# Outer magnitudes of an S4 kernel with their weights made as exponentials, and the angle of the weights from one arctangent

## The chip, the cores and the metric

The kernel runs on one core of a Trainium2 chip. The metric is device time in microseconds of one execution, the median over several runs. Five engines take part, each with an instruction stream of its own: PE (matrix products), DVE (vector work), ACT (functions of one argument and copies), POOL and SP. SP issues most of the transfers here, POOL the rest. An engine works through its own instructions in order and waits at an instruction until what it depends on is done.

## The reference, cut to what matters

One block of a network on a sequence x of L = 2048 rows with D = 512 channels. Six vectors come from a condition c; the first half of the block is a long convolution, the second a token mixer with an MLP.

```
mod = (silu(c) @ w_mod)                        # 512 -> 6 x 512: sa, ca, ga, sb, cb, gb
h = layernorm(x) * (1 + ca) + sa
dt = exp(log_dt);  A = A_re + 1j * A_im        # A: 512 x 128
P = exp((dt * A)[:, :, None] * arange(2048))   # 512 x 128 x 2048, complex
K = einsum("dn,dnl,dn->dl", C, P, dt * B).real # 512 x 2048, summed over n = 128
y = irfft(rfft(pad(h.T)) * rfft(pad(K)))[:, :2048].T + h * Dskip
x = x + ga * y
h = layernorm(x) * (1 + cb) + sb
x = x + gb * mixer_mlp(h)                      # w1, shifts by 1 and 2 rows, w2; w3, gelu, w4
```

The change concerns how K is made. K[d, l] = Re of the sum over n of W exp(dt A l), with the weight W = C B dt.

## The kernel before, in words

**How K is tiled.** The exponent is split as l = 64 b + a: an inner factor exp(dt A a) with 64 values of a, and an outer one, W exp(64 dt A b), with 32 values of b. For 16 channels at a time, K is then a set of small products over n (128 rows) of an outer tile e1 (32 columns a channel, real and imaginary part) and an inner tile e0. The 512 channels make 32 steps k of 16 channels; eight blocks t of four steps u, with `t, u = divmod(k, 4)`.

**What a step needs.** Each complex factor is a magnitude times a sine or cosine.

- `turns(k, cos)` makes the phase in turns of both factors as a product on PE (four matmul pairs for the sine, five for the cosine, each on 64 rows, a column range for the inner and one for the outer factor). Tables of constants (C0, C1) multiply rows that hold the phase of each channel, split into a high and a low part (T0S inner, T1S outer). Adding and taking off a large number inside the product (the tiles ON and MG) removes the whole turns. One ACT operation with the table of sines then gives `sn` or `cs`, 128 x 1024.
- `exps(t, u0, u1)`, once a block, makes the magnitudes: four exponentials of 128 x 1024 for the inner factor (p0, one for each step of the block, from TES, the rows of dt A_re), and one of 128 x 768 (p1) that holds for each channel a table of 8 and one of 4 outer exponentials.
- `weigh(t)` multiplies p1's tables of 4 by the magnitudes of the weights, WN, on DVE.
- `products(k)`, on DVE: m1 (the outer magnitude, 16 x 32, as a product of the tables of 8 and 4), e0 from sn, cs and p0 (three operations), e1 from sn, cs and m1 (two operations).
- `burst(k, e0, e1)`: 64 small matmuls that sum over n. Every second step ACT copies the result to KX.

**The loop** runs over k = 0 to 32. In step k the program issues the turns of step k + 2, evictions left from the step before, then the products and the burst of step k. In steps with k % 4 == 1 (called fresh here) the exponentials of the next block come in between: ACT changes its table from sines to exponentials and back there (ACT_TABLE_LOAD). `fill` issues matmuls whose result isn't used, to keep PE at work. Beside this, the loop normalizes x (u_stats, u_norm), takes its short transforms (`u_dft`: 8 matmuls, then two ACT evictions to vs, then transfers to VU by SP), and makes the modulation vectors 3 to 5 (`mod_parts`, `mod_sum`).

**The preparation** in front of the loop: dt; the rows la = dt A_re and tf (phase in turns), split into high and low parts (hilo; `hi` on ACT, `lo` on DVE); `place` and `parts`, products with the placing matrices PA and PB that move the rows to where the loop's products want them (TES, T0S from PA; T1S from PB); the weights wr + i wi = C B; their angle by the arctangent of the smaller over the larger of |wr| and |wi|, with corrections for octant and signs on DVE (at); their magnitude from the sine of that arctangent and a second reciprocal (wn), transposed on PE to WN; and modulation vectors 0 to 2. `load_mod(n)` loads a block of w_mod by SP into one of two buffers "xu", the third block into the buffer of the first; ACT scales it, PE sums it over 128 rows, ACT copies the result (modu).

**What sets the order.** All of this is written out by hand (`manual_schedule`): each engine takes its instructions in the order in which the program issues them. Buffers come from pools. There are two PSUM buffers of 1024 columns for sines, cosines and exponentials alike (xx), two for u_dft and modulation (pu), two for kp.

**Behind the loop**: the skip weights Dskip, loaded into DS at the start, are added to K (`KX`), KX is multiplied by FK (`k_first`), and spectrum, inverse transform and MLP follow. Vs, VU and the loads `ld` are x's way there.

Of the kernel before, what the change touches and what calls it, by code (L numbers as in the profile page):

```python
# [7 lines left out]
F32 = mybir.dt.float32  # L8
# [14 lines left out]
NX0 = 64  # L23
NX1 = 12
NXC = 16 * NX0 + 64 * NX1


def shape_constants():
# [24 lines left out]
    for hh in range(2):  # L53
        for c2 in range(2):
            for cc in range(16):
# [14 lines left out]
    ex1 = np.concatenate([64 * np.arange(8), 512 * np.arange(4)])  # L70
    CE = np.concatenate([(eye[:, :, None] * ex0.reshape(2, 32)[:, None, None, :]).transpose(1, 0, 2, 3).reshape(16, -1),
                         np.zeros((16, 64 * NX1))], 1)
    CE = np.tile(CE, (8, 1))
    for u in range(4):
        CE[u * 32:u * 32 + 32, 1024 + u * 16 * NX1:1024 + (u + 1) * 16 * NX1] = \
            np.tile((eye[:, :, None] * ex1).reshape(16, -1), (2, 1))
    PA = np.zeros((2, 4, 16, 2, 2, 4, 2, 16))
    PB = np.zeros((4, 2, 16, 4, 4, 2, 4, 16))
    for e in range(16):
# [9 lines left out]
        FI=FI.reshape(128, 16 * 128), C0=C0, C1=C1, CE=CE, PA=PA.reshape(128, 512), PB=PB.reshape(128, 2048), ID=np.eye(128)).items()}  # L89
# [20 lines left out]
def body(ctx, tc, A):  # L110
    nc = tc.nc
# [7 lines left out]

    VU = dpool.tile([2, 64, 64, 256], F32, name="VU")  # L120
# [65 lines left out]
    DS = ph.tile([128, 128], F32, name="DS")  # L186
# [5 lines left out]
    CE = ph.tile([128, NXC], F32R, name="CE")  # L192
# [6 lines left out]
    mods = [modu[:, k] for k in range(3)] + [modg[:, k] for k in range(3)]  # L199
# [39 lines left out]

    def exps(t, u0, u1):  # L240
        if u0 == 0:
            PE[t] = [], pe.tile([128, 4, 16, NX1], F32, name="p1")
        p0, p1 = PE[t]
        for u in range(u0, u1):
            x = psx.tile([128, 1024], F32, name="xx")
            if u == 4:
                for i, n in ((0, 512), (512, 64 * NX1)):
                    T.matmul(x[:, i:n], TES[:, t], CE[:, 1024 + i:1024 + n], start=True, stop=True)
                act(p1.rearrange("p u d c -> p (u d c)"), x[:, :64 * NX1], AF.Exp)
                continue  # L250
            l = TES[u * 32:u * 32 + 32, t]
            for i in range(2):
                T.matmul(x[:, i * 512:i * 512 + 512], l, CE[u * 32:u * 32 + 32, i * 512:i * 512 + 512],  # L253
                         start=True, stop=True)
            p0.append(pe.tile([128, 2, 512], F32, name="p0", bufs=6))
            act(p0[u].rearrange("p a b -> p (a b)"), x, AF.Exp)

    def weigh(t):
        q1 = PE[t][1][:, :, :, 8:12].rearrange("p a b c -> p (a b) c")
        V.tensor_mul(q1, q1, WN[:, t * 64:(t + 1) * 64, None].to_broadcast([128, 64, 4]))  # L260
# [9 lines left out]
    cst = pp.tile([128, 512], F32, name="cst")  # L270
# [3 lines left out]
    for k in ("ar", "ai", "cr", "br", "ci", "bi"):  # L274
        raw[k] = pp.tile([128, 4, 128], F32, name="raw_" + k)

# [4 lines left out]
    with tc.manual_schedule():  # L281
# [6 lines left out]
        for k, t in (("PA", PA.rearrange("p a b c -> p (a b c)")), ("CE", CE), ("C0", C0),  # L288
                     ("PB", PB.rearrange("p a b c -> p (a b c)")), ("C1", C1)):
            P.dma_start(t, A[k])  # L290
# [3 lines left out]
        V.memset(DS, 0.0)  # L294
        for j in range(4):
            Y.dma_start(DS[32 * j:32 * j + 1], A["dk"][j:j + 1])
        Y.dma_start(FK, A["FK"])
        V.memset(cst, MAGIC)
        for r in (32, 96):
            V.memset(cst[r:r + 32], 1.0)  # L300
        V.tensor_copy(MG, cst)
        V.memset(cst[:, :384], 0.0)
        for i, (r, v) in enumerate(((0, 1.0), (0, -1.0), (32, 0.25))):
            for q in (r, r + 64):
                V.memset(cst[q:q + 1, i * 128:i * 128 + 128], v)
        V.tensor_copy(ON.rearrange("p a b -> p (a b)"), cst[:, :384])
# [3 lines left out]
        dtp = pp.tile([128, 4], F32, name="dtp")  # L310
        V.tensor_scalar(dtp, dt, INV2PI, None, op0=OP.mult)
# [13 lines left out]
        V.tensor_tensor(as4(la), raw["ar"], by(dt), op=OP.mult)  # L325
        hi(6, la)
        V.tensor_tensor(as4(tf), raw["ai"], by(dtp), op=OP.mult)
# [7 lines left out]
        V.tensor_scalar(ex[:, 4:], ex[:, 4:], 1.0, None, op0=OP.add)  # L335
        V.reciprocal(ex[:, 4:], ex[:, 4:])
        V.tensor_mul(scb, ex[:, 4:], cT)
# [5 lines left out]
        V.tensor_mul(t0, ci, bi)  # L343
        lo(2, t64)
        V.tensor_sub(wr, wr, t0)
# [3 lines left out]
        exps(0, 0, 5)  # L349
        act(C0N, C0.bitcast(F32), scale=-1.0)  # L350
        act(C1N, C1.bitcast(F32), scale=-1.0)
        px = [psx.tile([128, 1024], F32, name="xx") for i in range(2)]

        def parts(i0, i1):
            for v in range(4):
                for i in range(i0, i1):
                    T.matmul(px[v // 2][:, v % 2 * 512:v % 2 * 512 + 512], PB[:, v, i], hilo[:, 2 + i],
                             start=(i == 0), stop=(i == 3))

        parts(0, 2)  # L360
        ax, ay, mn = cr, br, tmp("mn")
# [41 lines left out]
        for i in range(4):  # L403
            s = slice(i * 128, (i + 1) * 128)
            T.transpose(wps[:, s], wn[:, s], ident)
# [636 lines left out]
```

## Time and profile before

| | us |
|---|---|
| median of 3 runs | 812.99 (812.83 to 813.55) |
| the profiled execution | 819.14 |
| its span in the profile | 817.4 |
| preparation | 0 to 42.6 |
| loop of 32 steps | 42.6 to 257.6 |
| spectrum, inverse, mixer, MLP | 257.6 to 817.4 |
| busy over the span: PE | 725.9 (89%) |
| DVE | 511.1 (63%) |
| ACT | 339.0 (41%) |
| POOL | 92.5 (11%) |

The span is the stretch that the profiler recorded of one execution; the time of that execution holds 1.7 us more around it. Busy is the sum of an engine's instructions. The mean granted clock of PE over the span is 0.937 of full speed. Rows of the trace give the start in us, the duration in us, the engine, the line of the kernel, the operation with what it writes and reads, the shape, and in brackets how long the engine stood idle before it and what released it. Groups give the count, then busy time and mean in ns of one, then the idle time before them with the releaser. "PEld" is the load of the fixed operand of a matmul, "SPq" the issue of a transfer by SP. L118 is the helper that issues all of ACT's operations, so ACT's rows are told apart by their tiles.

### The profile page before, as it was taken

The page shows a single profiled execution, that of the slowest core. Times are in us where ns is not written, and L with a number is a line of the kernel's source. Part 1 is how long each engine was busy: PE and PEld are TensorE (multiplying, and loading weights), DVE is VectorE, ACT ScalarE, POOL GpSimd, SP SyncE. Part 2 cuts the span into 40 slices and gives each one's busy share as a digit, 9 for nine tenths or more (in the row PEclk, how much of TensorE's full clock was granted, in tenths as well). Part 3 has the DMA queues.
Part 4 walks back from the last instruction along what each step waited for, and adds up shares of the span by engine and source line. Part 5 has one row for each costly group of instructions (what it writes and reads, how often), then busy time and mean ns, then how long its engine had stood idle before and what let it go on. Part 6 is the DMA issues. An engine that isn't in the chain of part 4 may idle for free. (4 is left out here: it accounts for less than half of the span.)

```text
span 817.4 us, 17349 instructions
## 1 busy us (share of the span) xinstructions
PE 725.9 (89%) x7340; PEld 550.9 (67%) x7340; DVE 511.1 (63%) x883; ACT 339.0 (41%) x540; POOL 92.5 (11%) x186
## 2 busy tenths in 40 slices
PE   3798999889888989999459899999999999999994
PEld 1355555545556956565248788888888888888883
DVE  8999888768765355777479988543526271714211
ACT  3677676656755344453134554221322122222220
POOL 1011111011000000010026331010101010101000
PEclk9999999989998599999769899999999999999997
DMA  8421152421415999495803453010101010101011
GB/s 294 147 53 41 26 145 53 116 68 28 117 40 131 246 250 311 146 307 182 287 1 121 160 177 118 26 53 1 52 1 53 1 52 1 26 1 26 1 26 26
DMA packets 51046, 79.88 MB, mean 98 GB/s; under 512 B 5172, under 2 KB 37816, under 8 KB 49432
## 3 DMA queue, kind: packets, MB, share of 16 engines
q1 hardware_dynamic: 44808, 57.92, 25.6%
q0 software_dynamic: 6160, 20.85, 8.1%
q8 instruction: 58, 0.95, 0.5%
q14 instruction: 20, 0.16, 0.1%
HBM read 52.53 MB, written 26.21 MB: 96 GB/s over the span
## 5 line engine op out<-in xcount | busy, mean ns | idle before, releaser
L871 DVE TENSOR_TENSOR gl<-gf,gh 128x512 fp32r<-128x512 f32 (+1 forms) x48 | 30.4, 644 | 150.5 <-ACT gh L118 150.5
L118 ACT ACTIVATE gf<-pm 128x512 f32<-128x512 f32 (+1 forms) x48 | 27.0, 562 | 182.1 <-PE pm L865 178.4
L865 PE MATMUL pm<-nh,w3l 128*128 128x256 f32 (+1 forms) x352 | 98.5, 280 | 0.0
L864 PE MATMUL pm<-nl,w3h 128*128 128x256 f32 (+1 forms) x352 | 98.5, 280 | 0.0
L863 PE MATMUL pm<-nh,w3h 128*128 128x256 f32 (+1 forms) x352 | 98.4, 279 | 0.0
L876 PE MATMUL pa<-w4h,gh 128*128 128x512 f32 (+1 forms) x176 | 73.8, 419 | 3.2 <-ACT gh L118 0.9
L877 PE MATMUL pa<-w4l,gh 128*128 128x512 f32 (+1 forms) x176 | 69.6, 396 | 0.0
L863 PEld LDWEIGHTS pm<-nh,w3h 128*128 128x128 f32 (+1 forms) x352 | 65.4, 186 | 1.8
L865 PEld LDWEIGHTS pm<-nh,w3l 128*128 128x128 f32 (+1 forms) x352 | 65.4, 186 | 1.1
L864 PEld LDWEIGHTS pm<-nl,w3h 128*128 128x128 f32 (+1 forms) x352 | 65.2, 185 | 0.6
L878 PE MATMUL pa<-w4h,gl 128*128 128x512 f32 (+1 forms) x176 | 64.2, 396 | 0.0
L481 DVE SCALAR_TENSOR_TENSOR e<-sn,p 128x512 f32<-128x512 f32 x64 | 41.3, 686 | 33.5 <-ACT sn L118 14.2
L461 PE MATMUL xx<-MG,ON 64*128 64x512 f32 x160 | 51.0, 416 | 0.0
L462 PE MATMUL xx<-MG,ON 64*128 64x512 f32 x160 | 50.9, 415 | 0.0
L118 ACT ACTIVATE sn<-xx 128x1024 f32<-128x1024 f32 x32 | 32.9, 1027 | 40.9 <-issue 34.4
L884 POOL DMA_DIRECT2D out<-KX x32 | 16.1, 508 | 257.6 <-DVE KX L882 257.5
L876 PEld LDWEIGHTS pa<-w4h,gh 128*128 128x128 f32 (+1 forms) x176 | 33.0, 188 | 17.9 <-ACT gh L118 13.2
L770 PE MATMUL pm<-nl,w1h 128*128 128x256 f32 x128 | 39.0, 305 | 6.6 <-DVE nl L741 6.6
L643 DVE TENSOR_TENSOR ma<-pk,us 128x512 f32<-128x512 f32 x32 | 21.9, 685 | 29.3 <-issue 21.3
L118 ACT ACTIVATE p<-xx 128x1024 f32<-128x1024 f32 (+1 forms) x40 | 37.8, 981 | 5.1 <-PE xx L253 3.3
L501 PEld LDWEIGHTS kp<-e,e 128*32 128x32 f32 x2048 | 30.5, 111 | 13.1 <-issue 8.5
L769 PE MATMUL pm<-nh,w1h 128*128 128x256 f32 x128 | 39.3, 307 | 0.0
(222 smaller groups left out, 1910.7 us busy)
## 6 DMA issues: line engine op xcount, KB each, us to landing
VU<-vs SPq DMA_DIRECT2D x64, 128.0 KB, 2.4
ld<-VU SPq DMA_DIRECT2D x32, 256.0 KB, 8.7
ZT<-z POOLq DMA_DIRECT2D x16, 512.0 KB, 4.4
ld<-ZT SPq DMA_DIRECT2D x16, 512.0 KB, 5.4
wst<-in_w SPq DMA_DIRECT2D x18, 256.0 KB, 3.3
xu<-in_u SPq DMA_DIRECT2D x16, 256.0 KB, 6.6
KX<-in_u SPq DMA_DIRECT2D x16, 256.0 KB, 9.7
GD<-go POOLq DMA_DIRECT2D x16, 256.0 KB, 3.3
```

The costliest lines, as they stand in the source:

```text
L118: return S.activation(out, in_, f, bias=bias, scale=scale)
L461: T.matmul(x[:, :512], la, ma, start=(i == 0), stop=(i == len(ops) - 1))
L462: T.matmul(x[:, 512:], lb, mb, start=(i == 0), stop=(i == len(ops) - 1))
L481: V.scalar_tensor_tensor(e0[:, 1, a], sn[:, 0], 1.0 - 2.0 * a, mg[:, a], op0=OP.mult, op1=OP.mult)
L769: T.matmul(p[:, e], W1h[:, k, c], hi[k], start=(k == 0), stop=False)
L770: T.matmul(p[:, e], W1h[:, k, c], lo[k], start=False, stop=False)
L863: T.matmul(p[:m, e], W3h[:, k, c], hi[k], start=(k == 0), stop=False)
L864: T.matmul(p[:m, e], W3h[:, k, c], lo[k], start=False, stop=False)
L865: T.matmul(p[:m, e], W3l[:, k, c], hi[k], start=False, stop=(k == 3))
L876: T.matmul(acc[i], gh[:m, e, s], W4h[:m, f], start=(f == 0), stop=False)
L877: T.matmul(acc[i], gh[:m, e, s], W4l[:m, f], start=False, stop=False)
L878: T.matmul(acc[i], gl[:m, e, s], W4h[:m, f], start=False, stop=(f == 10))
```

## The change

**Outer magnitudes.** The table of 8 and 4 goes. Instead the logarithm of the weight's magnitude, ln |W|, becomes rows of a product: a new tile TWS holds, in high and low parts, 64 dt A_re (for the outer position) and ln |W|, and its product with C1 (the constants that the outer phase uses too) is the logarithm of the whole weighted outer magnitude. Two more exponentials of 128 x 1024 a block (u = 4, 5) make it for four steps. m1 and `weigh` go, and e1 becomes a single product of 128 x 1024, for which sine and cosine lie in one tile `tr`. CE, the table of constants for the magnitudes, loses its last 768 columns.

**Angle.** arg W = 2 arctan(wi / (|W| + |wr|)), with the sign of wr handled by sw. |W| is exp(0.5 ln(|W| squared)); the same logarithm is ln |W|'s source. One reciprocal is left of three.

**Tables.** `table(i)` issues a load of ACT's table as an instruction of its own, in the place where the program has it. Before, the loads came where the builder put them: in front of the first operation that needs another table.

**Constants.** ON and MG are loaded by POOL as one tile MO instead of being written by memsets on DVE, and MG is one column that is read 512 times. POOL's order of loads changes.

**Order.** In the preparation, C0N, C1N, four of the first six exponentials and the modulation 0 to 2 come behind T1S. The tile of the skip weights, DS, moves behind the loop: a memset and four transfers.

```diff
+    def table(i):
+        S.add_instruction(mybir.InstLoadActFuncSet(name=nc.get_next_instruction_name(), act_func_set_id=i, ins=[], outs=[]))
+
+    LOG, EXP, TRIG = 5, 0, 9
...
-    MG = ph.tile([128, 512], F32R, name="MG")
-    ON = ph.tile([128, 3, 128], F32R, name="ON")
-    WN = ph.tile([128, 512], F32, name="WN")
-    modu = ph.tile([128, 3, 512], F32, name="modu")
...
+    MO = ph.tile([128, 392], F32R, name="MO")
+    ON = MO[:, :384].rearrange("p (a b) -> p a b", a=3)
+    MG = MO[:, 384:385].to_broadcast([128, 512])
+    modu = ph.tile([128, 2, 512], F32, name="modu")
...
     def exps(t, u0, u1):
...
             x = psx.tile([128, 1024], F32, name="xx")
-            if u == 4:
-                for i, n in ((0, 512), (512, 64 * NX1)):
-                    T.matmul(x[:, i:n], TES[:, t], CE[:, 1024 + i:1024 + n], start=True, stop=True)
-                act(p1.rearrange("p u d c -> p (u d c)"), x[:, :64 * NX1], AF.Exp)
-                continue
...
             for i in range(2):
...
+                if u < 4:
+                    r = slice(u * 32, u * 32 + 32)
+                    l, m = TES[r, t], CE[r, i * 512:i * 512 + 512]
+                else:
+                    r = slice(64 - i * 64, 128 - i * 64)
+                    l, m = TWS[r, t * 2 + u - 4], C1[r]
+                T.matmul(x[:, i * 512:i * 512 + 512], l, m, start=True, stop=True)
+            q = pe.tile([128, 2, 512], F32, name="p1" if u > 3 else "p0", bufs=4 if u > 3 else 6)
+            act(q.rearrange("p a b -> p (a b)"), x, AF.Exp)
+            (p1 if u > 3 else p0).append(q)
 
-    def weigh(t):
-        q1 = PE[t][1][:, :, :, 8:12].rearrange("p a b c -> p (a b) c")
-        V.tensor_mul(q1, q1, WN[:, t * 64:(t + 1) * 64, None].to_broadcast([128, 64, 4]))
...
+        act(s2, wr, AF.Square)
+        act(ax, wr, AF.Abs)
+        act(rw, wi, AF.Square)
...
+        V.scalar_tensor_tensor(s2, s2, 1e-37, rw, op0=OP.max, op1=OP.add)
+
+        act(s2, s2, AF.Ln)
+        table(EXP)
+        act(rw, s2, AF.Exp, scale=0.5)
+        V.tensor_add(rw, rw, ax)
+        V.reciprocal(rw, rw)
+        exps(0, 0, 2)
+        table(TRIG)
+        sw = t0
+        V.tensor_scalar(sw, wr, 0.0, -2.0, op0=OP.is_lt, op1=OP.mult)
+        V.tensor_mul(rw, rw, wi)
+        V.scalar_tensor_tensor(rw, sw, 1.0, rw, op0=OP.add, op1=OP.mult)
+        act(at0, rw, AF.Arctan)
...
+        parts(px4, (2, 3, 4, 5), 0, 2)
+        parts(pw4, (6, 7, 0, 1), 0, 2)
...
+        hi(4, ph1)
+        lw = t1
+        V.scalar_tensor_tensor(as4(lw), as4(s2), 0.5, by(ld[:, :4]), op0=OP.mult, op1=OP.add)
+        lo(4, ph1)
+        hi(0, lw)
+        lo(0, lw)
+        parts(px4, (2, 3, 4, 5), 2, 4)
+        table(EXP)
...
+        parts(pw4, (6, 7, 0, 1), 2, 4)
+        for v in range(4):
+            act(TWS.rearrange("p (t v) n -> p v t n", v=4)[:, v], pw4[v].rearrange("p (t n) -> p t n", t=4))
         act(C0N, C0.bitcast(F32), scale=-1.0)
         act(C1N, C1.bitcast(F32), scale=-1.0)
...
+        exps(0, 2, 6)
+        table(TRIG)
         mp = [mod_parts(n) for n in range(2)]
...
     def products(k):
...
-        m1 = wk1.tile([128, 16, 32], F32, name="m1")
-        V.tensor_mul(m1.rearrange("p d (x y) -> p d x y", x=4),
-                     pt[:, :, None, :8].to_broadcast([128, 16, 4, 8]),
-                     pt[:, :, 8:12, None].to_broadcast([128, 16, 4, 8]))
...
-        V.tensor_mul(f2(e1[:, 1]), sn[:, 1], f2(m1))
-        V.tensor_mul(e0[:, 0], cs[:, 0:1].to_broadcast([128, 2, 512]), mg)
-        V.tensor_mul(f2(e1[:, 0]), cs[:, 1], f2(m1))
+            V.scalar_tensor_tensor(e0[:, 1, a], tr[:, 1, 0], 1.0 - 2.0 * a, mg[:, a], op0=OP.mult, op1=OP.mult)
+        V.tensor_mul(e0[:, 0], tr[:, 0, 0:1].to_broadcast([128, 2, 512]), mg)
+        V.tensor_mul(e1.rearrange("p r d x -> p r (d x)"), tr[:, :, 1], m1[:, None, :].to_broadcast([128, 2, 512]))
...
                 if fresh:
+                    table(EXP)
                     exps(k // 4 + 1, 0, 2)
...
-                    for u in range(2, 5):
+                    for u in range(2, 6):
                         exps(k // 4 + 1, u, u + 1)
-                        fill(2)
-                if k % 4 == 3 and k < 28:
-                    weigh(k // 4 + 1)
+                        fill(2 - u // 4)
+                    table(TRIG)
...
+        DS = wml.tile([128, 128], F32, name="wm")
+        V.memset(DS, 0.0)
+        for j in range(4):
+            Y.dma_start(DS[32 * j:32 * j + 1], A["dk"][j:j + 1])
         V.tensor_add(Kq[:, :, :, 31], DS.rearrange("p (h g) -> p h g", h=2), Kq[:, :, :, 31])
```

In each of the following, a row is one instruction, or several alike (x2), with its line, what it writes and reads, and its shape.

ACT at the end of the preparation, from C1N to the first sine of the loop, before (tp_mn is the ratio of which the arctangent is taken, tp_wn the sine of it, hilo the high part of the angle, WN the weights' magnitudes, "xu<-pu" and "modu<-pu" the two halves of a modulation vector):

```order
L118 ACTIVATE C1N<-C_103 128x512
L118 ACT_TABLE_LOAD
L118 ACTIVATE tp_at_295<-tp_mn 128x512
L118 ACT_TABLE_LOAD
L118 ACTIVATE tp_wn<-tp_at_295,hpi 128x512
L118 ACTIVATE xu<-pu 128x512 x2
L118 ACTIVATE modu<-pu 128x512 x2
L118 ACTIVATE hilo<-tp_at 128x512
L118 ACTIVATE T1S<-xx 128x2x4x128 x2
L118 ACTIVATE WN<-pu 128x512
L118 ACTIVATE sn<-xx 128x1024
L118 ACTIVATE xu<-pu 128x512
```

And with the change, again from C1N to the first sine (p_315 to p_330 are four exponentials, of which the last two are outer magnitudes; C_102 is C1, ga the third modulation vector; T1S, four operations for TWS and C0N stand just ahead of the first row):

```order
L117 ACTIVATE C1N<-C_102 128x512
L117 ACTIVATE p_315<-xx 128x1024
L117 ACTIVATE p_320<-xx 128x1024
L117 ACTIVATE p_325<-xx 128x1024
L117 ACTIVATE p_330<-xx 128x1024
L121 ACT_TABLE_LOAD
L117 ACTIVATE xu<-pu 128x512 x2
L117 ACTIVATE modu<-pu 128x512
L117 ACTIVATE ga<-pu 128x512
L117 ACTIVATE xu<-pu 128x512
L117 ACTIVATE modu<-pu 128x512
L117 ACTIVATE tr<-xx 128x1024
```

The modulation vectors stood in front of the angle's high part (the third behind the first sine); now all three stand between the exponentials and the first sine.

ACT in the first fresh step of the loop, with what each instruction waits for, before:

```order
L118 ACT_TABLE_LOAD
L118 ACTIVATE p_547<-xx 128x1024 [waits PE_49]
L118 ACTIVATE p_552<-xx 128x1024 [waits PE_49]
L118 ACTIVATE p_602<-xx 128x1024 [waits PE_49]
L118 ACTIVATE p_609<-xx 128x1024 [waits DVE_49,PE_49]
L118 ACTIVATE p_543<-xx 128x768 [waits PE_49]
L118 ACT_TABLE_LOAD [waits PE_49]
L118 ACTIVATE sn<-xx 128x1024 [waits Activation_49]
```

And with the change:

```order
L121 ACT_TABLE_LOAD
L117 ACTIVATE p_536<-xx 128x1024 [waits PE_49]
L117 ACTIVATE p_541<-xx 128x1024 [waits PE_49]
L117 ACTIVATE p_588<-xx 128x1024 [waits PE_49]
L117 ACTIVATE p_595<-xx 128x1024 [waits DVE_49,PE_49]
L117 ACTIVATE p_602<-xx 128x1024 [waits PE_49]
L117 ACTIVATE p_608<-xx 128x1024 [waits PE_49]
L121 ACT_TABLE_LOAD
L117 ACTIVATE tr<-xx 128x1024 [waits DVE_49,PE_49,Activation_49]
```

The wait for PE moved from the second table load to the sine behind it, and there is one exponential more.

SP's transfers at the end of the loop, before (in_wm is w_mod, in_T the table T2, "ld<-VU" the first loads of x's spectrum):

```order
L210 DMA wm<-in_wm 128x4x512
L447 DMA VU<-vs 64x2x256 x20
L558 DMA xu<-in_T 128x2048
L598 DMA ld<-VU 64x4x256 x2
```

And with the change (in_dk are the skip weights, in the buffer "wm"):

```order
L214 DMA wm<-in_wm 128x4x512
L437 DMA VU<-vs 64x2x256 x20
L546 DMA wm<-in_dk 1x128 x4
L549 DMA xu<-in_T 128x2048
L589 DMA ld<-VU 64x4x256 x2
```

Four small transfers stand between the last ones of vs and the load of T2; before they stood near the start of the queue.

More of the change, by code (lines that the diff above doesn't have):

```diff
@@ L293, in body @@
         load_mod(1)
-        V.memset(DS, 0.0)
-        for j in range(4):
-            Y.dma_start(DS[32 * j:32 * j + 1], A["dk"][j:j + 1])
         Y.dma_start(FK, A["FK"])
[L298 to L306, printed above, removed]
+        table(LOG)
         V.tensor_scalar(ld[:, 4:], cT, -1.0, None, op0=OP.mult)
@@ L351, in body @@
         act(C1N, C1.bitcast(F32), scale=-1.0)
[L352 to L361, printed above, removed]
-        V.scalar_tensor_tensor(ax, wr, -1.0, wr, op0=OP.mult, op1=OP.max)
@@ L449, in u_dft, with turns, turn @@
         later.append(evict)
-    def turns(k, cos):
+    def turns(k):
+        o = wk.tile([128, 2, 2, 512], F32, name="tr", bufs=3)
+        for cos in range(2):
+            turn(k, cos, o[:, 1 - cos])
+        return o
+    def turn(k, cos, o):
         t, u = divmod(k, 4)
```

122 lines of the change are left out of this document (44 added, 78 removed).

## The prediction

> **What bounds the kernel now.** I read first the table by stretches, to see where the stages that the change touches begin and end, then the engine rows inside them, then the order of instructions on either side of the change.
>
> The table by stretches (columns: stretch, its length, then busy time and count of PE, PEld, DVE, ACT, POOL, the granted TensorE clock, DMA share, GB/s), and the row that places the 32 bursts:
>
> ```profile
> 0.00:42.60 42.60, 23.44 (x84) 12.37 (x84) 37.39 (x84) 21.92 (x29) 3.18 (x10) 0.96 0.66 212
> 42.60:257.60 215.00, 191.47 (x2923) 117.52 (x2920) 172.67 (x264) 144.14 (x167) 20.12 (x32) 0.94 0.28 68
> L501 PE MATMUL kp<-e,e x2048: 219/219/314, 49.1 to 257.4; 128*32 128x64 f32 x187
> ```
>
> So there are three parts: a preparation of 42.6 us, the loop of 32 steps (215 us, 6.7 us a step), and 560 us behind it that the change doesn't edit. In the loop DVE is busy for 172.7 of 215 us and PE for 191.5, whose ends are modelled. What a step asks of PE is read from starts:
>
> ```profile
> 213.84 0.50 PE L461 MATMUL xx<-C,T0S 64*128 64x512 f32 x1
> ...
> 216.10 1.10 PE L501 MATMUL kp<-e,e 128*32 128x64 f32 x64
> 217.13 1.09 PE L438 MATMUL pu<-xu,FU 32*64 32x512 f32 x8
> 218.15 0.49 PE L461 MATMUL xx<-C,T0S 64*128 64x512 f32 x1
> ```
>
> A pair of turns takes 2.26 us, a burst 1.03, a DFT of u 1.02, back to back. Where PE stands still in the loop, the groups of the stretch 42:258 tell (behind the second bar: idle time before the group, and who ended it):
>
> ```profile
> L438 PE MATMUL pu<-xu,FU 32*64 32x512 f32 x128 | 23.8, 640 | 10.4 <-ACT vs L118 9.0 <-ACT modg L118 1.5
> L253 PE MATMUL xx<-CE,TES 32*128 32x512 f32 x56 | 20.6, 446 | 6.1 <-ACT cs L118 3.3 <-ACT p L118 2.3 <-ACT sn L118 0.3
> L217 PE MATMUL pu<-wm,scb 128*32 128x512 f32 x24 | 3.3, 628 | 3.9 <-ACT vs L118 3.9
> ```
>
> These are 20.4 us, and ACT ends all of it. The mean clock of 0.94 means that about 2 x 0.06 x 215 = 26 us passed at half clock, 13 us lost. That leaves some 180 us of PE work at full clock. PE sets the loop's pace, held up by ACT; DVE does not. DVE is what the change relieves most.
>
> The stall that the change does reach is the table load behind the exponentials (ACT and PE, in time):
>
> ```profile
> 203.16 1.28 ACT L118 ACT_TABLE_LOAD   x1 [2.74 <-PE xx L462]
> 204.46 1.02 ACT L118 ACTIVATE sn<-xx 128x1024 f32<-128x1024 f32 x1
> ...
> 206.85 1.10 ACT L118 ACTIVATE vs<-pu 128x512 f32<-128x512 f32 x2
> 204.15 1.10 PE L501 MATMUL kp<-e,e 128*32 128x64 f32 x64
> 207.51 1.57 PE L438 MATMUL pu<-xu,FU 32*64 32x512 f32 x8 [2.27 <-ACT vs L118]
> ACT L118 <- PE xx L462: 16.7, 7, 2.8
> ```
>
> ACT idles 2.74 us for the sine's matmuls and only then loads the table: the load carries the sine's wait. Everything behind it is 1.28 us later, up to the eviction of vs, for which PE stands 2.27 us. The last row, of the waits, counts seven such stalls.
>
> **The loop, part by part.** DVE loses the product m (L477) and weigh (L260), and two products of e1 become one:
>
> ```profile
> L477 DVE TENSOR_TENSOR m<-p 128x512 f32<-128x512 f32 x30 | 20.2, 674 | 0.3
> L260 DVE TENSOR_TENSOR p<-p,WN 128x256 f32<-128x256 f32 x8 | 3.4, 422 | 6.2 <-ACT p L118 4.9 <-ACT WN L118 1.2
> ```
>
> That is 23.6 us of DVE work, with some 2 us from the merged product. I count it at nothing but 0.6 (one m) at the last step, where no PE work is left to hide DVE: before that PE's own 180 us cover it. ACT gets two exponentials of 1024 for one of 768, some 1 us more in each of seven blocks of four steps, but its idle 16.7 us had room for it. PE gets two pairs of matmuls on 64 rows instead of two on 128 rows; I take 0.3 us a block, +2 in all (bounds 0 and 4). The loads have no wait of their own now. Each runs while PE still makes the sine's product, so ACT starts the sine about 1.3 us earlier, less about 0.2. Where a DFT or a mod product hangs on it (I count four of seven blocks) PE gets back some 1.1 us, elsewhere 0.3: -5.3. Half clock: the stretch right behind the stall at 207.51 ran at 0.51,
>
> ```profile
> 209.50:213.00 3.50, 3.50 (x30) 2.32 (x30) 0.38 (x1) 1.15 (x2) 0.00 (x0) 0.51 0.66 130
> ```
>
> and a shorter stall may spare it. I put a third of the 13 us lost down to such stalls: -4 (bounds 0 and -13). Loop: +2 - 5.3 - 0.6 - 4 = -8 (bounds -2 and -18).
>
> **The preparation.** ACT's chain is followed with these durations:
>
> ```profile
> 12.83 4.09 PE L322 MATMUL pu<-hilo,PA 128*128 128x512 f32 x8 [12.83 <-DMA PA<-in_PA]
> 16.96 0.60 ACT L118 ACTIVATE T0S<-pu 128x512 fp32r<-128x512 f32 x1 [0.26 <-PE pu L322]
> 21.50 3.35 DVE L367 RECIPROCAL tp_mx<-tp_mx 128x512 f32<-128x512 f32 x1
> 23.26 1.05 ACT L118 ACTIVATE C0N<-C 128x1024 fp32r<-128x1024 f32 x1
> 24.21 0.62 ACT L118 ACTIVATE C1N<-C 128x512 fp32r<-128x512 f32 x1
> 33.77 0.63 ACT L118 ACTIVATE hilo<-tp_at 128x512 fp32r<-128x512 f32 x1 [1.80 <-DVE tp_at L279]
> 34.43 0.69 DVE L316 TENSOR_TENSOR hilo<-tp_at,hilo 128x512 fp32r<-128x512 f32 x1 [0.69 <-ACT hilo L118]
> 35.18 3.14 PE L357 MATMUL xx<-hilo,PB 128*128 128x512 f32 x7 [0.23 <-DVE hilo L316]
> 41.54 1.02 ACT L118 ACTIVATE sn<-xx 128x1024 f32<-128x1024 f32 x1
> ```
>
> The removed memsets let DVE start as soon as cT lands; that gains nothing, since the placing matmuls wait for PA until 12.83 in both kernels and ACT's squares stand behind T0S, which ends at 17.56. From there: three ACT operations (0.63 each, neighbours overlapping by 0.1 as C0N and C1N do) to 19.2; a DVE operation (0.69), Ln (0.63), load (1.28), Exp (0.63), sum (0.69) to 23.3; reciprocal 3.35 to 26.6; three DVE operations to 28.3; arctangent to 29.0; DVE meanwhile prepares the phase to 30.5; one product to 31.2. The high part of the phase comes at 31.2 instead of 33.77: 2.5 us gained by the shorter chain for the angle.
>
> Then ACT has more in front of the first sine. Low parts and the second pair to 33.3; the product to 34.3 at full clock (35.8 at half, as the 3.14 for seven shows); T1S twice 1.02, then the new TWS four times 0.55, to 37.9; C0N and C1N, which stood at 23.26 beside other work, to 39.4; four exponentials on 128x1024 (1.02 as the sine, less the overlap), of which before none stood here, to 43.1; the load to 44.4. Against before that is 11 us of ACT work moved in front of the sine. Now the modulation, which before ran under the angle's chain:
>
> ```profile
> 30.52 0.39 SPq L210 DMA_DIRECT2D xu<-in_wm  x1
> xu<-in_wm SPq DMA_DIRECT2D x1, 1024.0 KB, 5.5
> 40.94 1.06 PE L217 MATMUL pu<-xu,scb 128*32 128x512 f32 x8
> 43.10 1.12 PE L224 MATMUL pu<-xu,sp 128*128 128x512 f32 x2
> 44.26 0.60 ACT L118 ACTIVATE modu<-pu 128x512 f32<-128x512 f32 x1 [0.22 <-PE pu L224]
> ```
>
> The third block of w_mod takes the buffer of the first, so it is asked for only after the first sum. That is at 30.52 before, and its 5.5 us (second row) lie under the angle's chain. Now the two partial sums reach ACT at 44.4 to 45.5, the first sum is through at about 46, the load lands at about 51.5, and in the built order ACT has the third block's xu and modu in front of the first sine, where before the sine came first. So 51.5 + 1.06 + 0.6 + 1.12 + 0.6 = 55: the first sine at about 55.5 instead of 41.54. Both PE and ACT are empty meanwhile but for the first turns. Preparation: +14 (bounds +11, if hand-overs are tighter, and +17, if the products run at half clock). The queues that the load passes hold only the loads of u behind it, not needed before the first statistics.
>
> Two more table loads stand in this chain than before, counted at 1.28 each. [...]
>
> [...]
>
> **Behind the loop.** The skip weights DS are loaded at the start now, unseen. They move behind the last vs in SP's queue, and the sum into KX waits for them:
>
> ```profile
> 8.77 1.75 SPq L296 DMA_DIRECT2D DS<-in_dk x4
> cT<-in_c SPq DMA_DIRECT2D x1, 2.0 KB, 1.7
> 258.48 0.61 SPq L447 DMA_DIRECT2D VU<-vs  x1
> 258.32 0.42 DVE L556 TENSOR_TENSOR KX<-DS,KX 128x128 f32<-128x128 f32 x1 [1.85 <-ACT KX L118]
> 258.80 0.33 PE L585 MATMUL pk<-FK,KX 32*128 32x64 f32 x2 [1.17 <-DVE KX L556]
> ```
>
> Counted from the same loop end: SP is free at 259.09, four issues to 260.84, the last small transfer lands 1.7 later (as cT's), at 262.5; the sum starts there instead of at 258.32, and PE's first matmul behind it: +4.2. The load of T2 behind it in the queue is 1.75 later only. I take +4.2 (bounds +2, if the transfers behind take some of it up, and +5). The memset for it, behind the last product, lies under SP's issues.
>
> **Sum.** +14 - 8 + 4.2 = +10.2 us. The profiled execution took 819.1 (span 817.4); 829.3 there. The runs' median is 6 us lower, 813.0, so I forecast 823.2.
>
> **Rivals.** (1) *DVE paces the loop after all.* For it: its 172.7 busy us of 215. Against: the idle rows above, where ACT ends PE's waits. Then the loop falls by DVE's own 25.6 us less 2 for PE: +14 - 23.6 + 4.2 = -5.4, 807.6, faster. It decides once the loop gives back over 18.2 us. Chance 0.14.
> (2) *The third block's load isn't in front of the sine*, because it starts earlier than I think; then the sine starts after the table load, at about 46: +4.5 instead of +14, and the sum is +0.7, 813.7. Against: the built order and the buffer. Chance 0.06.
> (3) *The broadcast operand is slow.* MG is now one element read 512 times by five of the nine matmul pairs of a step (2.26 / 9 = 0.25 us a pair). At half rate: 32 x 5 x 0.25 = +40, 863. Broadcast weights give no hint of it:
>
> ```profile
> L490 PEld LDWEIGHTS kp<-CE,TES 128*128 128x128 f32 x12 | 2.0, 188 | 1.1 <-issue 0.7
> L224 PEld LDWEIGHTS pu<-xu,sp 128*128 128x128 f32 x6 | 1.0, 188 | 3.4 <-ACT xu L118 3.1 <-issue 0.2
> ```
>
> The second loads a broadcast column, at 188 ns like the first. The moving side isn't shown. Chance 0.06.
>
> **Chances.** My forecast has 0.74, with 816 to 831 as its own range (a gain in the loop of 2 to 15, the bounds of preparation and tail nearly offsetting). The range 807 to 836 takes in rival 1 and leaves out rival 3. A change under 0.2% (1.6 us) can't be told from none here. Faster 0.15, from rival 1 and a little of the rest; same 0.06, mostly rival 2; slower 0.79.
>
> **What would show it.** Right: the first sine at 53 to 58 with ACT idle some 5 us for the load of w_mod; the bursts' span from 208 us to about 200; table loads before sines with no idle before them; PE idle for KX behind the loop for over 4 us. Wrong: a first sine before 50, a loop under 195 us, or MG matmuls further than 0.25 us apart.

## The result, and the profile after

The changed kernel takes 840.04 us (median of 4 runs, 839.53 to 845.45) against 812.91 for the kernel before: ratio 1.0347 (1.0305 to 1.039). In a second series it took 839.33 (median of 4) against 815.47 (23 runs of the kernel before, 810.2 to 821.3): ratio 1.0258 (1.020 to 1.032). The forecast was 823.2, with a range to 836: the right direction, and 16.8 us too low. All ratios in this document leave out runs marked slow, over 1.5% above the fastest of the same kernel (two of e5's twelve, two of e6's ten, four of e9's twelve; none of the kernel before), which flatters those three: with all twelve runs e9's median is 815.37 against 816.27.

The table by stretches, after (columns as before; preparation, loop to the start of the last burst, what follows):

```profile
0.00:57.40 57.40, 28.25 (x100) 14.11 (x100) 24.73 (x60) 29.82 (x41) 3.69 (x11) 0.85 0.49 154
57.40:273.00 215.60, 196.49 (x2870) 118.40 (x2870) 148.99 (x194) 153.00 (x174) 18.30 (x32) 0.92 0.28 66
273.00:838.20 565.20, 512.42 (x4400) 421.48 (x4400) 301.50 (x537) 173.24 (x345) 69.40 (x144) 0.93 0.34 100
```

The first sine comes at 57.4 instead of 41.5. The loop is as long as before (215.6 against 215.0) although DVE is busy 24.6 us less in it. The same stretch before:

```profile
41.50:256.50 215.00, 191.50 (x2869) 117.06 (x2861) 173.56 (x265) 145.24 (x169) 20.12 (x32) 0.94 0.28 67
```

In time, the end of the preparation and the end of the loop:

```profile
32.73 1.94 ACT L117 ACTIVATE T1S<-xx 128x1024 fp32r<-128x1024 f32 x2
...
37.92 3.89 ACT L117 ACTIVATE p<-xx 128x1024 f32<-128x1024 f32 x4
41.83 1.28 ACT L121 ACT_TABLE_LOAD   x1
45.87 0.37 SPq L214 DMA_DIRECT2D xu<-in_wm  x1
52.06 1.94 PE L221 MATMUL pu<-xu,scb 128*32 128x512 f32 x8 [3.81 <-DMA xu<-in_wm]
54.10 0.60 ACT L117 ACTIVATE xu<-pu 128x512 f32<-128x512 f32 x1 [6.76 <-PE pu L221]
56.86 0.60 ACT L117 ACTIVATE modu<-pu 128x512 f32<-128x512 f32 x1 [2.17 <-PE pu L228]
57.36 1.02 ACT L117 ACTIVATE tr<-xx 128x1024 f32<-128x1024 f32 x1
...
269.89 7.89 SPq L437 DMA_DIRECT2D VU<-vs  x8
272.99 1.08 PE L489 MATMUL kp<-e,e 128*32 128x64 f32 x58 [0.48 <-DVE e L472]
277.88 1.31 SPq L546 DMA_DIRECT2D wm<-in_dk  x4
280.30 0.42 DVE L547 TENSOR_TENSOR KX<-wm,KX 128x128 f32<-128x128 f32 x1 [7.23 <-DMA wm<-in_dk]
280.78 0.47 PE L576 MATMUL pk<-FK,KX 32*128 32x64 f32 x2 [6.19 <-DVE KX L547]
```

The third block of w_mod is asked for at 45.87 and read at 52.06; ACT stands 6.76 and 2.17 us for it with the first sine behind. At the end DVE stands 7.23 us for the skip weights, whose transfers SP issues only at 277.88, behind eight of vs at 1 us each. In the kernel before the last eight of vs took 5.70 us:

```profile
253.38 5.70 SPq L447 DMA_DIRECT2D VU<-vs  x8
```

PE's groups in the loop, after:

```profile
L457 PE MATMUL xx<-MO 64*128 64x512 f32 x155 | 48.2, 410 | 0.0
L428 PE MATMUL pu<-xu,FU 32*64 32x512 f32 x128 | 23.8, 642 | 6.9 <-ACT vs L117 6.6 <-ACT modg L117 0.2
L258 PE MATMUL xx<-CE,TES 32*128 32x512 f32 x56 | 21.4, 461 | 5.9 <-ACT tr L117 3.4 <-ACT p L117 2.3
L221 PE MATMUL pu<-wm,scb 128*32 128x512 f32 x24 | 3.2, 604 | 3.0 <-ACT vs L117 3.0
```

The idle time in front of the transforms of u fell from 10.4 to 6.9 us. One of the loads behind the exponentials, where ACT now waits for the sine's matmuls after the load and no longer before it:

```profile
188.90 1.28 ACT L121 ACT_TABLE_LOAD   x1
193.97 1.02 ACT L117 ACTIVATE tr<-xx 128x1024 f32<-128x1024 f32 x1 [3.79 <-issue]
```

The broadcast MG costs nothing: 410 ns a matmul, against 415 before:

```profile
L462 PE MATMUL xx<-MG,ON 64*128 64x512 f32 x156 | 49.6, 415 | 0.0
```

What took the gain back is the clock:

```profile
176.50:179.91 3.41, 2.79 (x71) 1.81 (x70) 3.30 (x5) 3.38 (x4) 0.00 (x0) 1.00 1.07 336
179.91:193.57 13.66, 13.66 (x36) 5.95 (x37) 3.96 (x6) 6.60 (x7) 1.45 (x2) 0.50 0.33 84
```

Half clock for 13.66 us in one fresh step.

### The profile page after: what moved, and what is told of

Its sections match the earlier page's. It is cut to its first block, busy times and chain, and to the rows that moved or that the text cites. A ratio compares the mean times of both kernels' runs of the same rounds, so it can differ in the third digit from the quotient of the medians.

```text
span 838.2 us, 17314 instructions
## 1 busy us (share of the span) xinstructions
PE 737.2 (88%) x7368; PEld 554.0 (66%) x7368; DVE 475.2 (57%) x790; ACT 356.1 (42%) x558; POOL 91.4 (11%) x187
## 5 line engine op out<-in xcount | busy, mean ns | idle before, releaser
L470 DVE SCALAR_TENSOR_TENSOR e<-tr,p 128x512 f32<-128x512 f32 x64 | 41.3, 686 | 64.1 <-ACT tr L117 56.1
L117 ACT ACTIVATE tr<-xx 128x1024 f32<-128x1024 f32 x32 | 32.8, 1025 | 50.1 <-issue 43.1
L117 ACT ACTIVATE p<-xx 128x1024 f32<-128x1024 f32 x48 | 47.1, 1026 | 7.2 <-PE xx L258 6.3
L457 PE MATMUL xx<-MO 64*128 64x512 f32 x160 | 49.6, 409 | 0.0
L458 PE MATMUL xx<-MO 64*128 64x512 f32 x160 | 49.6, 409 | 0.0
L867 PEld LDWEIGHTS pa<-w4h,gh 128*128 128x128 f32 (+1 forms) x176 | 33.0, 187 | 17.8 <-ACT gh L117 13.3
L472 DVE TENSOR_TENSOR e<-tr,p 128x1024 f32<-128x1024 f32 x32 | 39.0, 1218 | 0.0
L471 DVE TENSOR_TENSOR e<-tr,p 128x1024 f32<-128x1024 f32 x32 | 39.0, 1218 | 0.0
```

The lines of the kernel that those rows point to most:

```text
L117: return S.activation(out, in_, f, bias=bias, scale=scale)
L457: T.matmul(x[:, :512], la, ma, start=(i == 0), stop=(i == len(ops) - 1))
L458: T.matmul(x[:, 512:], lb, mb, start=(i == 0), stop=(i == len(ops) - 1))
L470: V.scalar_tensor_tensor(e0[:, 1, a], tr[:, 1, 0], 1.0 - 2.0 * a, mg[:, a], op0=OP.mult, op1=OP.mult)
L471: V.tensor_mul(e0[:, 0], tr[:, 0, 0:1].to_broadcast([128, 2, 512]), mg)
L472: V.tensor_mul(e1.rearrange("p r d x -> p r (d x)"), tr[:, :, 1], m1[:, None, :].to_broadcast([128, 2, 512]))
```

## The experiments

Each trace is taken apart in the same way: the loop runs from the first sine to the start of the last burst; "half clock" is half of the time in it that the clock's records show at 0.50; "idle" is the sum of the gaps between PE's matmuls; "work" is what is left, an estimate of PE's work at full clock. "Tail" is from the start of the last burst to the first matmul of k_first, "rest" what follows.

| kernel | first sine | loop | half clock | idle | work | tail | rest | ratio of times to before |
|---|---|---|---|---|---|---|---|---|
| before | 41.5 | 215.0 | 11.9 | 23.5 | 179.6 | 2.3 | 558.6 | |
| before, again (e7) | 41.7 | 210.8 | 6.8 | 23.9 | 180.1 | 2.3 | 554.9 | |
| changed | 57.4 | 215.6 | 16.9 | 19.2 | 179.5 | 7.8 | 557.4 | 1.0347 (1.0305 to 1.039) |
| changed, again (e8) | 55.2 | 216.6 | 17.5 | 19.4 | 179.7 | 6.7 | 561.5 | 1.0258 (1.0201 to 1.0316) |
| e1 | 57.8 | 213.5 | 14.1 | 19.3 | 180.1 | 2.3 | 555.5 | 1.0242 (1.0201 to 1.0282) |
| e2 | 51.6 | 210.5 | 10.2 | 18.4 | 181.9 | 6.1 | 557.1 | 1.0106 (1.0055 to 1.0157) |
| e3 | 53.7 | 207.8 | 6.8 | 18.8 | 182.2 | 2.3 | 558.4 | 1.0063 (1.0023 to 1.0102) |
| e4 | 61.1 | 211.6 | 5.7 | 24.3 | 181.6 | 7.8 | 559.0 | 1.0353 (1.0317 to 1.0389) |
| e5 | 48.1 | 207.7 | 6.8 | 18.7 | 182.2 | 2.8 | 557.7 | 0.9974 (0.9937 to 1.0011) |
| e6 | 46.4 | 208.5 | 6.8 | 19.5 | 182.2 | 2.3 | 559.3 | 0.9973 (0.9936 to 1.0011) |
| e9 | 42.5 | 211.6 | 8.5 | 19.7 | 183.4 | 2.7 | 555.6 | 0.9951 (0.9909 to 0.9993) |
| e9, again (e12) | 42.4 | 207.1 | 3.4 | 19.6 | 184.1 | 2.3 | 555.7 | 1.0000 (0.9973 to 1.0028) |
| e10 | 42.6 | 212.1 | 30.7 | 28.9 | 152.5 | 2.3 | 558.1 | 0.9999 (0.9974 to 1.0024) |
| e11 | 41.8 | 202.2 | 3.4 | 18.7 | 180.1 | 2.3 | 558.0 | 0.9912 (0.988 to 0.9944) |

**e1: the skip weights at the start again.**

```diff
-        DS = wml.tile([128, 128], F32, name="wm")   # behind the loop, with its 4 transfers
+    DS = ph.tile([128, 128], F32, name="DS")        # at the start, behind load_mod(1)
```

> The changed kernel with the skip weights loaded at the start again. Theory (their four transfers behind the last vs in SP's queue hold up the sum into KX, and everything behind waits): the time from the last burst's start to the first matmul of k_first falls from 7.8 to about 2.3 us, as before the change, and the whole from 840 to about 834.5. Rival (the loads of VU behind take up most of the wait): the first matmul comes 5.5 us earlier, but PE then idles for the first loads of VU, and the whole falls by under 2 us, to 838 to 840.

End of the loop in its trace:

```profile
273.13 0.42 DVE L547 TENSOR_TENSOR KX<-DS,KX 128x128 f32<-128x128 f32 x1 [1.85 <-ACT KX L117]
273.61 0.33 PE L576 MATMUL pk<-FK,KX 32*128 32x64 f32 x2 [1.17 <-DVE KX L547]
```

The tail is 2.3 us again, and the rest did not grow (555.5 against 557.4 and 561.5). So the move cost 5.5 us in the first trace of the changed kernel and 4.4 in its second. The whole, 835.1, is near the 834.5 expected, but the times alone don't show the gain: 1.0242 lies beside 1.0258 of the changed kernel on that chip.

**e2: the first two modulation sums in front.**

```diff
         act(at0, rw, AF.Arctan)
+        mp = [mod_parts(n) for n in range(2)]   # both sums, load_mod(2) and load_u(0);
...                                              # taken out behind exps(0, 2, 6)
```

> The changed kernel with the first two modulation sums (and so the request for the third block of w_mod) directly behind the arctangent, where the kernel before had them; the third sum stays behind the exponentials. Theory (the late third block holds the first sine): the block is asked for at about 31 us and lies ready when ACT reaches it; the first sine starts at 45 to 47 us instead of 57.4, and the stretch of half clock from 50 to 64 us goes, which is worth some 3 us more in the first steps: 840 falls to 825 to 829. Rival (ACT's own work in front of the sine is what holds it, the block only fills the rest): the first sine still comes after 52 us and the whole falls by under 6 us.

The block is asked for at 31.47. ACT in this trace:

```profile
37.73 1.96 ACT L117 ACTIVATE T1S<-xx 128x1024 fp32r<-128x1024 f32 x2 [1.73 <-PE xx L320]
...
48.15 0.60 ACT L117 ACTIVATE xu<-pu 128x512 f32<-128x512 f32 x1
51.11 0.60 ACT L117 ACTIVATE modu<-pu 128x512 f32<-128x512 f32 x1 [2.37 <-PE pu L228]
51.60 1.02 ACT L117 ACTIVATE tr<-xx 128x1024 f32<-128x1024 f32 x1
```

Neither side was right. The wait for the block is gone (48.15 has no idle time), but the sums now push T1S back by 5 us (37.73 against 32.73) and the third sum still stands in front of the sine: 51.6, not 45 to 47. The block's lateness alone is worth 5.8 us (3.6 against the second trace of the changed kernel); the other 10 us to the kernel before are, by these rows, ACT's work and waits in front of the sine. Yet the whole fell by some 15 us on that chip (823.95 against 839.33), in part since the loop lost less to half clock as well (10.2 against 17.5).

**e3: both edits.**

> Both of the edits above together. If preparation and tail are separate places: the gains add up, 840 - 13 - 5.5 = about 821.5. What then is left against 813 is 3 to 4 us of preparation and the loop, in which the change gained nothing. Rival (the loop is faster once it begins at full clock): under 816.

822.65 against 821.5 expected, but not by the sum expected: beside e2 (823.95) the early skip weights bring only 1.3 us, within the spread. The tail is whole again (2.3 against 6.1 in e2); the first sine, at 53.7, is 2.1 later than in e2 and still 12 us late.

**e4: no table loads of its own** (`table` does nothing; loads stand where the first operation needs them).

> The changed kernel without table loads of its own, so that each load stands in front of the first operation that needs the table and carries that operation's waits. Theory of the prediction (own loads are hidden in ACT's wait for the sine's matmuls): a row of about 1.3 us comes back behind every sine wait in fresh steps, four of seven of them in front of an eviction that PE waits for, and the load in front of the first sine comes back too: 840 rises by 5 to 7 us. Rival (PE's fillers and clock take up the difference, the loads are worth nothing): within 1.5 us of 840.

```profile
220.48 1.28 ACT L117 ACT_TABLE_LOAD   x1 [2.40 <-issue]
221.77 1.02 ACT L117 ACTIVATE tr<-xx 128x1024 f32<-128x1024 f32 x1
```

The load waits and then stands in front of the sine again, as in the kernel before. PE's idle time in the loop goes from 19.2 to 24.3 us: the hidden loads are worth 5.1 us, as predicted (5.3). The first sine is 3.7 us later. The time (843.5) is 3.5 to 4.2 us above the changed kernel's two medians, less than the 5 to 7 expected, and single runs overlap: this loop lost only 5.7 us to half clock.

**e5: the preparation rebuilt.** The main edits:

```diff
-    LOG, EXP, TRIG = 5, 0, 9
+    LOG, EXP, TRIG = 6, 0, 9        # one table with ln and exp: table(EXP) behind Ln goes
-        exps(0, 0, 2)
+        exps(0, 0, 4)
+        mod_parts(0)()
+        g0 = mod_sum(0)
+        load_mod(2)
...
-        act(C0N, C0.bitcast(F32), scale=-1.0)
+        P.tensor_scalar(C0N, C0.bitcast(F32), -1.0, None, op0=OP.mult)
```

> The change with its preparation put in another order: skip weights at the start; one table that holds both ln and exp in place of two; four exponentials of the inner factor under DVE's reciprocal instead of two; the phase's products on DVE in front of the reciprocal; the first modulation sum (and the request for the third block) in front of the arctangent; C0N and C1N on POOL; the placing for TWS behind that for T1S. Theory (the angle's chain is shorter than before the change, and what holds the first sine is only the work that stands in front of it): request for the third block at about 25 us, first sine at 39 to 42 us against 41.5 in the kernel before, loop shorter by 4 to 5 us of PE idle, so 810 to 814 against 816.5 in the same runs, faster by 0.3 to 0.8%. Rival (TWS and the modulation can't be hidden, the first sine stays behind 45): 817 or more, not faster.

```profile
20.87 0.63 ACT L117 ACTIVATE raw_cr<-raw_cr 128x512 f32<-128x512 f32 x1 [0.76 <-DVE raw_cr L354]
21.54 0.63 ACT L117 ACTIVATE raw_br<-raw_cr 128x512 f32<-128x512 f32 x1
...
34.53 0.60 ACT L117 ACTIVATE xu<-pu 128x512 f32<-128x512 f32 x1 [3.80 <-PE pu L222]
48.13 1.02 ACT L117 ACTIVATE tr<-xx 128x1024 f32<-128x1024 f32 x1
```

ln and exp follow each other without a load (20.87 and 21.54), from one table; in the changed kernel a load of 1.28 us at 19.46 lies between them. The rival's first sine came true: 48.1. The angle's chain began 2.1 us later than in the changed kernel (ln at 20.87, there at 18.81), the block was asked for at 29.95 instead of 25, and ACT stands 3.80 us for PE in front of the second block's scaling. Against the kernel before no difference can be measured: 6.6 us lost in the preparation, and a loop shorter by 7.3 us than in its first trace, by 3.1 than in its second.

**e6: DVE's relief taken back.** To the kernel of e5:

```diff
+        V.tensor_mul(e1[:, 0].rearrange("p d x -> p (d x)"), tr[:, 0, 1], m1)
         V.tensor_mul(e1.rearrange("p r d x -> p r (d x)"), ...)
```

> The same kernel with half of the product e1 done twice: one more DVE product of 128x512 a step, 32 x 0.69 = 22 us of DVE work, about what the change took off DVE. Theory (PE paces the loop; what DVE does is hidden): the loop gets longer by 0.7 us (the last step) to 3 us. Rival 1 of the prediction (DVE's work sets the loop's pace): longer by over 15 us.

The loop's stretch in e5 and in e6 (third pair: DVE):

```profile
48.10:255.90 207.80, 189.09 (x2877) 114.18 (x2875) 148.88 (x193) 152.96 (x174) 18.68 (x32) 0.97 0.29 69
```

```profile
46.40:254.90 208.50, 189.04 (x2873) 114.08 (x2869) 170.52 (x225) 152.95 (x174) 19.54 (x32) 0.97 0.29 69
```

21.6 us more of DVE, the loop 0.8 us longer, the same ratio. These 22 us of DVE's work in the loop are worth under 1 us, and rival 1 falls.

**e7 and e8: both kernels once more.**

> The kernel before, once more, for a second trace. If the stretches of half clock are set by the program, they stand in the same steps as in the first trace and the loop loses 11 to 13 us to them again. If they fall by chance on top of the program's stalls, some stand elsewhere and the loop's loss differs by several us, while PE's idle time in the loop stays at 23 to 24 us and its work at full clock at 180.

> The changed kernel, once more, on the chip of the other runs. First sine at 57 to 58 us, PE idle in the loop for 19 us, work at full clock 180 us. If half clock falls by chance, the loop's loss to it is not 16.9 us again but anything from 6 to 17, and the loop is then up to 8 us shorter than in the first trace; if the program sets it, 16 to 18 again.

Stretches of the clock in the first trace of the kernel before, and in its second (last figures: clock, DMA share, GB/s):

```profile
83.26:86.67 3.41, 3.41 (x9) 2.36 (x8) 3.41 (x6) 1.93 (x3) 0.86 (x1) 0.50 0.19 40
110.56:113.98 3.42, 3.42 (x10) 2.20 (x9) 1.44 (x3) 1.66 (x2) 0.00 (x0) 0.50 0.68 189
```

```profile
83.26:86.67 3.41, 3.41 (x18) 2.27 (x18) 3.41 (x6) 2.07 (x3) 0.97 (x2) 1.00 0.13 26
144.13:147.54 3.41, 3.41 (x18) 1.95 (x14) 3.26 (x7) 0.28 (x1) 0.00 (x0) 0.50 0.02 5
202.16:208.98 6.82, 6.82 (x42) 3.62 (x46) 2.22 (x3) 1.58 (x3) 0.00 (x0) 0.50 0.79 214
```

Same program, other stretches: idle and work agree within 0.5 us, half clock costs 11.9 or 6.8. The changed kernel's second trace, though, has two of its stretches where the first has them, among them 13.64 us in the same fresh step; its others stand elsewhere, and its first sine came at 55.2, not at 57 to 58:

```profile
175.60:189.24 13.64, 13.64 (x34) 5.99 (x36) 4.08 (x6) 6.72 (x7) 1.45 (x2) 0.50 0.29 75
```

So both expectations were half right: where a stretch falls differs between executions, and the late start goes with a larger loss in three of four traces (16.9, 17.5, 14.1; e4, with 5.7, is the fourth). It isn't chance alone, though. e1 has the stretches of 6.83 and 13.66 us of e8, both 42 and 120 us behind the first sine, and e3, e5 and e6 all have the same three: 3.41, 6.83 and 3.41 us at 57, 67 and 163 us behind it (the longest from 120.84, 115.49 and 113.67). In these groups the stretches start alike, to 0.2 us, behind the first sine. A loss that depends on where between two such starts the loop begins would fit this; no run here sets that, so it is not shown.

**e9 and e12: the preparation taken further.** To e5: squares in front of the placing for TES, both scalings of w_mod in front of the arctangent, the third sum behind the first two steps' turns.

```diff
+        mod_parts(2)()
+        mod_sum(2)()
+        load_u(1)
+        side[0].insert(0, lambda: V.tensor_mul(mods[0], mods[0], mods[2]))
```

> The rebuilt preparation taken further: the squares of the weights on ACT in front of the placing for TES, both scalings of w_mod in front of the arctangent, both modulation sums behind T1S, the third one behind the first two steps' sines (its only reader, the normalization of u, comes after step 0). Theory (the first sine is held only by what stands in front of it on ACT): first sine at 39 to 43 us against 48.1 in the first rebuilt version, loop as there (207 to 208 us at a half-clock loss of 6.8), so 6 to 9 us below that version: 807 to 810, faster than the kernel before by 0.6 to 1.1%. Rival (the third sum only moves the wait into the first steps, where products or normalization then stand still): first burst no earlier than 51 us and the whole within 2 us of the first rebuilt version.

First sine at 42.5, as expected, but the rival came true for the whole, which is no faster than the kernel before: 0.9951 and, repeated as e12, 1.0000. The third sum now stands in the first steps (first burst at 50.9 us, against 49.1 in the kernel before).

**e10: no fillers** (`fill` does nothing, in the kernel of e9).

> The same without the 84 matmuls that only keep PE at work (fill does nothing); their result is not used. If PE's own work sets the loop's pace and the fillers stand in front of it: the loop falls by up to the 30 us that they take. If ACT sets the pace in the fresh steps (two tables, six exponentials: 2 x 1.28 + 6 x 1.02 = 8.7 us, seven times) and the fillers only lie in its shadow: PE's idle time rises by 15 to 30 us instead, the loop stays within 3 us or gets longer where half clock follows.

The loop's stretch in e9 and in e10:

```profile
42.40:254.00 211.60, 191.89 (x2880) 114.19 (x2878) 148.92 (x193) 154.32 (x176) 18.75 (x32) 0.96 0.28 68
```

```profile
42.50:254.60 212.10, 183.28 (x2796) 109.66 (x2794) 148.90 (x193) 153.58 (x176) 18.74 (x32) 0.86 0.29 68
```

84 matmuls fewer, 31 us less work, and the loop as long as before: half clock took 22 us more and idle time 9 (15 to 30 were expected). The fillers cost about what they save: 815.83 us without them, 815.37 and 816.10 with them.

**e11: the kernel before, with own loads in the loop alone.**

```diff
+    def table(i):
+        S.add_instruction(mybir.InstLoadActFuncSet(name=nc.get_next_instruction_name(), act_func_set_id=i, ins=[], outs=[]))
...
                 if fresh:
+                    table(EXP)
                     exps(k // 4 + 1, 0, 2)
...
                         fill(2)
+                    table(TRIG)
```

> The kernel before with one part of the change alone: own table loads around the exponentials in the loop's seven fresh steps; magnitudes, weights, angle, preparation and tail as before. Theory (the hidden load is all that the loop of the changed kernel gains): PE's idle time in the loop falls from 23.5 to 18 to 19.5 us, first sine and tail stay at 41.6 and 2.3 us, and the whole is 4 to 5 us shorter: ratio 0.994 to 0.995. Rival (the gain needs the relief of DVE too, since the products wait for DVE behind the sines): PE's idle time stays above 22 us and the ratio at 0.998 to 1.002.

> The last rebuilt version of the change once more, beside the one above. If both have the same loop gain and nearly the same first sine (42.5 against 41.7), their ratios agree within 0.3%, and all that the exponential weights bring beyond the loads is nothing. Rival (the shorter DVE work and the shorter angle pay somewhere): this one is below the other by over 0.4%.

Groups of the loop in e11's trace:

```profile
L442 PE MATMUL pu<-xu,FU 32*64 32x512 f32 x128 | 22.9, 613 | 7.6 <-ACT vs L118 7.2 <-ACT modg L118 0.4
L221 PE MATMUL pu<-wm,scb 128*32 128x512 f32 x24 | 3.2, 604 | 2.7 <-ACT vs L118 2.7
```

808.67 against 815.77 us: ratio 0.9912, the only kernel here clearly faster than the kernel before, and 0.9% below e12 in the same series. Neither side of e12's expectation came true. Idle time falls by 5 us (10.4 to 7.6 and 3.9 to 2.7 in these groups). The loads pay without any of the new arithmetic. The time fell by 7 us, more than the 4 to 5 expected; the 2 beyond the idle time are within what the clock moves (half clock took 11.9 and 6.8 us in the two traces of the kernel before, 3.4 here).

## Why the prediction was right or wrong

From profile to profile the forecast was +10.2; measured, 840.03 - 819.14 = +20.9.

- **Preparation**: +14 predicted, +15.8 measured, by the steps named: T1S, TWS and exponentials 1.3 to 1.6 us ahead of their places, a lead lost again in the two sums, the block asked for at 45.87, the sine at 57.36 against 55.5. The matmuls behind the load ran slow (1.94 for eight and 2.08 for two, against 1.06 and 1.12 before), at a granted clock of 0.50. That is the miss; the prediction has half clock in its bound of +17 and not in its +14. Rival 2 is refuted.
- **Loop**: -8 predicted, +0.6 measured. This is the step that failed, and in it one term: half clock, put at -4, was +5.0 (16.9 against 11.9). I took half clock for a consequence of PE's stalls, so fewer stalls had to mean less of it. The stalls shrank as predicted (idle 23.5 to 19.2; -4.3 against -5.9 with the last step) and half clock grew. 3.2 us of the 16.9 are the tail of the stretch that began in PE's wait for w_mod (50.2 to 63.9). For the rest, what sets off a stretch isn't settled: the longest gap between PE's matmuls in this loop is 1.6 us, against 2.27 before, and in the 13.66 us of the stretch at 179.91 PE is busy throughout. So the cause of the larger loss stays open.
- **Work**: +2 predicted. In the changed kernel's traces what is left is 179.5 and 179.7, no more than before; in e2 to e6 it is 181.6 to 182.2, which is +2 against 180. Both groups have as many matmuls of the turns in the loop, to one pair. What differs is half clock, and half of the time overstates what it costs: the nine pairs of matmuls of a step's turns take 4.00 us at a clock of 0.50 (from 58.43 to 62.43), against the 2.26 of the prediction's rows, 1.8 times as long. By that, an estimate, the 16.9 us are 15 and the 11.9 before 10.6. So some of the work is hidden in the column beside it, and up to a microsecond of the miss may be work and not clock; half clock grew all the same.
- **DVE at nothing**: right (e6).
- **Behind the loop**: +4.2 predicted, +5.5 measured, above the bound of +5: SP needed 1 us for each transfer of vs there (7.89 for eight, against 5.70) and came to the skip weights 4.9 us after the last burst's start, not 2.6. In the second trace it was +4.4.
- **From profile to median**: -6 was wrong. The first three runs of the kernel before lay low; over 15 to 23 runs its median is 815.5 to 816.5, and 819.1 is within its spread (810 to 821). A single profile needs no such correction when nothing says that profiling costs time: the changed kernel's profile, 840.03, is its median.
- **Rival 3** is refuted by the 410 ns.

The misses add up: 1.8 (preparation) + 8.6 (loop) + 1.3 (tail) - 1.2 (rest, 557.4 against 558.6) = 10.5 of the 10.7 us, and the 6 us of the median on top.

## What to carry to other kernels

Taking 22 us off an engine that waits was worth nothing here, and work moved in front of the first instruction of the bounding loop delayed the loop by 15.8 us: follow what each queue now has to finish before that instruction, transfers included. Take a change apart before judging it: here one small part (table loads of their own, issued while the engine waits) was worth 0.9%, and no version with the arithmetic that came with it was faster than the kernel before. When a clock that varies from run to run costs 3 to 17 us of a loop, compare idle time and work from traces beside the times, and many runs, not three.

## What the runs showed of the hardware

- Half clock comes in these traces in stretches whose length and distance are multiples of 3.41 us (3.41, 6.82, 13.66; 83.26 to 110.56 is 8 times 3.41), with a start that differs between executions of one kernel (83.26 in the first trace of the kernel before and 144.13 in its second are 17.8 times 3.41 apart). The two traces of the kernel before, 819.14 and 811.47 us, differ by 5.1 us in the loop's half clock, so the spread of 10 us between runs of one kernel can in part come from there.
- Fillers cost about as much as they save here (e10): the loop takes 212.1 us without them, 211.6 and 207.1 with them.
- Half clock doesn't double the time of every matmul here: in the changed kernel a step's turns take 4.00 us at 0.50, against 2.26 at 1.00 in the kernel before, and fillers in a row start 0.43 or 0.59 us apart against 0.23 or 0.34.
- A clock of 1.00 in the table by stretches can mean that nothing was recorded. In e5, eight placing matmuls behind a short wait, the same later, and the clock of the first stretch:

```profile
28.93 4.40 PE L324 MATMUL xx<-hilo,PB 128*128 128x512 f32 x8
...
38.16 2.03 PE L324 MATMUL kp<-hilo,PB 128*128 128x512 f32 x8
```

```profile
28.90:33.20 4.30, 4.30 (x10) 2.62 (x8) 1.98 (x3) 1.30 (x3) 0.00 (x0) 1.00 0.44 130
```

The clock's records of this trace begin only at 33.57 us, and time without a record counts as 1.00. So the slow matmuls stand where the clock isn't known; the later ones, 2.03 us for eight, stand where it is recorded as 1.00. In the changed kernel eight placing matmuls from 22.35 us take 3.78 us at a recorded 0.50, and seven from 31.58 us take 1.90 us at 1.00.
